# Gated attention and a token/channel mixer on one core: the mixer's work for each batch put into two stretches of fixed contents

## The chip, the cores and the metric

The kernel runs on one core of one Trainium2 chip. A core has five engines with instruction queues of their own: PE (TensorE, matmuls into PSUM), ACT (ScalarE), DVE (VectorE), POOL (GpSimd) and SP (SyncE, which here issues DMAs alone), and 16 DMA engines that all queues share. PSUM is held as bank pairs, of which this kernel uses four in turn. The metric is the time of one execution in microseconds (us) on the device; smaller is better.

## The reference

Eight batches of 3008 rows, 256 wide; z has 64 columns, w_tok1 leads from 3008 rows to 256 tokens and w_tok2 back, w_ch1 leads from 256 to 1536 channels and w_ch2 back.

```python
# for each batch
scores = (1.0 / S) * z @ z.T              # S = 3008
attn   = np.maximum(scores, 0.0) ** 2
x      = u * (attn @ v)
h      = np.maximum(x.T @ w_tok1, 0.0) @ w_tok2
u2     = x + h.T
out    = u2 + np.maximum(u2 @ w_ch1, 0.0) @ w_ch2
```

Each batch's mixer needs the x of the whole batch (x.T @ w_tok1 sums over all rows), so the mixer of a batch can begin only when its attention is finished; the attention of the next batch doesn't wait for it.

## The kernel before

**Tiles and blocks.** The rows of a batch b are cut into six query blocks q of 512 rows (the last has 448), and into six key groups g of four tiles of 128. A block (b, q) needs the squared scores of its six groups. scores are symmetric, so a block that lies above the diagonal is computed once and turned for its mirror: `flips` (L275) says which, `flip` (L515) issues the DMA transpose on SP (L518) from an at tile into an fl tile. From batch 2 on, the diagonal block is scored as a triangle and completed by three small transposes (`flip_tiles`, L508, L511). There are six at buffers and ten fl buffers.

**Attention on PE.** Scores (`score_run`, L424) have 64 rows of contraction, and the product with v (`av_matmul`, L646) is cut into two halves of 64 rows, so both run as two row tiles side by side in the array. ACT applies the relu (`relu`, L450 and L462), DVE squares (`square`, L470; L499 for triangles). At a block's end `finish` copies one half of the sum (ACT, L771), adds the other (DVE, L777), and `gate` (L787) multiplies by u, turned by SP beforehand (L228): that is x, transposed (xT, L798 and L803). `turn_x` (L809, issue at L811) turns it on SP for the mixer.

**The mixer on PE.** Its matmuls use the whole array of 128 rows. For a batch it is cut into pieces (`add_mixer`, L834): six of tok1 (L851, result a_ps, which read x), six of tok2 (L870, h_ps), then 36 of ch1 (L911, hp; four matmuls each, put out to h2pre by ACT at L925 or by DVE at L927) and 23 or 24 of ch2 (L955, op; twelve matmuls each). DVE adds the residual (L971, L989) and SP writes the result out (L976, L992). The residual needs u2 turned by SP (L893). tok1 and tok2 pieces lie in a list `heads`, ch1 and ch2 pieces in a list `tails`; a batch's pieces are added to both lists when its last block ends.

**The order.** It is written out by a planner in the kernel's own Python, before anything runs: a loop (from L1260) keeps an assumed clock for PE and for ACT, DVE and SP, and decides at each step what PE takes next: scores, an attention half, or a mixer piece (L1310 to L1336, else the earliest, L1337 to L1345). What the other engines do is kept in lists (`push`) with an assumed ready time, busy time and latency, and each engine's queue is the order in which the planner takes them. On the chip all queues run in that order and wait for each other by semaphores.

Before the change, a mixer piece is chosen by a budget: time spent on attention earns mixer time (`per_batch`, `flat`, `SLOW`, L1371), pieces spend it, and the run may be overdrawn by `SWING`. A mixer run starts between two blocks, at even q alone, and lasts until the budget is spent or no piece is ready; where none is ready, PE takes scores or an attention half.

**Loads.** POOL issues them. From batch 1 on, u, v and z loads are asked for at fixed steps of the attention (`at_group`, L1112; the step is counted in groups) and let out one by one (`ask_some`, L1123), at least `SPACING` = 4.5 us of assumed PE time apart. Ahead of each stands a one-element copy (`after`, L120) from a recent result, which holds POOL's queue until PE's work has come as far as that. z loads of the next batch are asked for at steps 14 to 19 of 36, v loads from step 28 on. When the third and the sixth z load is out, the turning of z on SP (L137, L141) is put into a list `later`, which u's turns share and which is worked off from its head.

Of the kernel before, what the change touches and what calls it, by code (L numbers as in the profile page):

```python
# [44 lines left out]
class Piece:  # L45


    def __init__(self, cost, needs, fn, opens=False, closes=False, room=None,
                 urgent=False):
        self.cost, self.needs, self.fn = cost, needs, fn  # L50
        self.opens, self.closes, self.room = opens, closes, room
        self.urgent = urgent


@with_exitstack
def kernel(
# [12 lines left out]
    B, S, D = u.shape  # L69
# [398 lines left out]
    def square(unit, view, t):  # L468
        (b, q, g), pr = unit
        nc.vector.tensor_mul(view, view, view)  # L470
        if (b, q, g) in early:
            for e in early[b, q, g][2 * pr:2 * pr + 2]:
                e.t = t
            if pr == 0:
                blocks[b, q, g] = (
                    Done(t), ats[b, q, g].rearrange("p (i w) -> p i w", w=QW), "at", [1])
            else:
                ats.pop((b, q, g))
            return
# [12 lines left out]
        recent[0] = at[:, :1]  # L492
# [212 lines left out]
    def do_half(start, g):  # L705
# [81 lines left out]
    def gate(blk, dh, acc, t):  # L787
# [46 lines left out]
    def add_mixer(b):  # L834
# [164 lines left out]
        for q in range(NQ):  # L999
            heads.append(Piece(0.874, [x_done[b, NQ - 1]], lambda end, q=q: tok1(q, end),  # L1000
                               opens=q < NQ - 1, closes=q > 0))
        for q in range(NQ):
            heads.append(Piece(4 * column_time(widths[q]), [a_done, tok2_done[q]],
                               lambda end, q=q: tok2(q, end)))
        def add_ch1(q, c2):
            h2_done[q, c2] = Done()
            tails.append(Piece(4 * column_time(widths[q]), [u_done[q]] + w_done[:2],
                               lambda end: ch1(q, c2, end),
                               room=("h2", "us") if c2 == 0 else ("h2",)))

# [12 lines left out]
        def add_ch2(q, half, i):  # L1023
            two = not alone(q, half)
            needs = [Sooner(h2_done[q, c2], 0.218 * c2) for c2 in range(CHT // 2)]
            tails.append(Piece(1.312, needs + w_done[2:],
                               lambda end: ch2(q, half, i, end), opens=two and i == 0,
                               closes=two and i == 1))


        early = ROOM["h2"] - CHT // 2
        for q in range(NQ):
            for c2 in range(early if q else 0, CHT // 2):
                add_ch1(q, c2)
            if q + 1 < NQ:
                for c2 in range(early):
                    add_ch1(q + 1, c2)
            for half in halves(q):
                for i in range(pieces_of(q, half)):
                    add_ch2(q, half, i)  # L1040

    def next_piece(t):
# [71 lines left out]

    asks, later = [], []
    last_ask = [0.0]
# [22 lines left out]
    def z_then_turn(b, j):  # L1139
        load_z(b, j)  # L1140
        if j % 3 == 2:
            later.append((pe[0] + 11.0, lambda: True, lambda: turn_next_z(b - 1, j // 3)))

    for b in range(B):
        base = b * NQ * NG
# [8 lines left out]
        if b + 1 < B:  # L1154
            at_group(base + NG, lambda b=b: new_zT(b + 1))
            for j, c in enumerate(vorder):
# [72 lines left out]

    per_batch = 0.87 * NQ * (2 + CHT // 2) + 1.35 * 4 * NQ  # L1230
    flat = NQ * NG * 1.73 + NQ * (NQ + 1) / 2 * 0.44
    fill(7, bank_pair(0, "wp")[:, 0, :])
# [15 lines left out]
    first_u(18.5)  # L1248

    done_units = 2  # L1250
    budget = 8.0
    NOW = 0.05
    STARVED = 0.7
    BACKLOG = 0.9
    GRAIN = 2
    SWING = 2.0
    SPACING = 4.5
    SLOW = 0.84
    LONG = 12.0
    while cur[0] is not None or heads or tails:  # L1260
        run_engines(pe[0])
        ask_some()
        t = pe[0]
        ta, g = next_half(t)
        tm, pieces = next_piece(t)
        blk = cur[0]

# [34 lines left out]

        between = blk is None or blk.acc[0] is None
        mixer_now = tm <= t + NOW and (budget > -SWING or blk is None)
        pick = None
# [31 lines left out]
        if pick is None:  # L1337
            options = [(ta, "av"), (tm, "mixer")]
            if n_now and (whole or low if runs else spare):
                options.append((ts, "scores"))  # L1340
# [26 lines left out]
        else:  # L1367
            if not pieces[0].urgent:
                budget -= pieces[0].cost
            do_piece(tm, pieces)  # L1370
        if pick != "mixer" and blk is not None and blk.b >= 1:  # L1371
            budget += per_batch * (pe[0] - t) / flat * (SLOW if blk.b == 1 else 1.0)
    run_engines(FAR)
# [30 lines left out]
```

## Time and profile before

| what | us |
|---|---|
| median of 3 runs | 1148.66 |
| lowest and highest of them | 1147.0, 1149.11 |
| the profiled execution's own time | 1146.15 |
| its span, first to last instruction | 1144.4 |
| PE busy | 1134.3 |
| DVE busy | 638.4 |
| ACT busy | 548.9 |
| POOL busy | 153.6 |

The page and the views of the trace describe one execution. A row of a group has the line, the engine, the operation, its tiles and shape and its count, then busy time and the mean of one in ns, then the idle time of the engine ahead of it. PE's matmuls overlap and their ends are modelled, so the mean of one (374 ns for 512 columns) is a latency and not a price; starts tell the price. A few matmul records are missing from the trace (for instance 1106 of 1152 at L911), while all weight loads are there.

From the groups, in ns: a relu of a score unit at L462 takes 1028 (a triangle's, in smaller pieces, 441 at L450), a square 687, ch1's evacuation 999 on ACT and 1211 on DVE, the copy at a block's end 579, the add 676, the gate 665, the residual 692.

PE alternates between attention stretches of two blocks and mixer stretches: for batch 4, for instance, an attention stretch runs from 602.4 to 624.05, a mixer stretch to 646.6, an attention stretch to 670.6, a mixer stretch to 696.2. The program ends with one mixer stretch of about 100 us, from 1039.1 on, which holds the rest of batch 6 and all of batch 7.

### The profile page before, as it was taken

Reading aid. Unit: us, or ns where it says so; the run is one execution under the profiler, and the core shown is the slowest. Engines: PE = TensorE matmul, PEld = TensorE weight load, DVE = VectorE, ACT = ScalarE, POOL = GpSimd, SP = SyncE. Lnnn points to the kernel's source line nnn. Section 1 sums busy time; section 2 is a strip of 40 time slices with the busy share of each in tenths; the row PEclk is TensorE's granted clock in tenths of the full one; section 3 lists DMA queues with packets and bytes.
Section 4 is the critical chain, followed back from the end, with each engine's and each line's share of the span. In section 5 each row is a group of like instructions: output and inputs, shape, how many; then the busy total and the mean of one; then the engine's idle time right before and its main releaser. Section 6 shows DMA issues by size and latency. Waiting matters only on the chain.

```text
span 1144.4 us, 22411 instructions
## 1 busy us (share of the span) xinstructions
PE 1134.3 (99%) x9160; PEld 673.0 (59%) x9219; DVE 638.4 (56%) x947; ACT 548.9 (48%) x699; POOL 153.6 (13%) x387
## 2 busy tenths in 40 slices
PE   9999999999999999999999999999999999999998
PEld 3455465645557566565565655665566556566666
DVE  6888454465553755537546375554644656434544
ACT  7998534374352752526525354344543554412331
POOL 4500110210111001111011100111002110000000
PEclk9999999999999999999999999999999999999999
DMA  9999964975879858799688996899867997742122
GB/s 159 191 171 230 164 120 97 203 138 118 170 120 197 164 114 157 132 198 161 122 150 141 186 176 111 152 140 189 164 126 140 151 183 149 121 103 56 51 84 65
DMA packets 468199, 164.85 MB, mean 144 GB/s; under 512 B 431936, under 2 KB 445824, under 8 KB 468096
## 3 DMA queue, kind: packets, MB, share of 16 engines
q1 hardware_dynamic: 440240, 130.72, 57.9%
q0 software_dynamic: 27344, 32.32, 20.9%
q8 instruction: 72, 1.18, 0.4%
q10 hardware_dynamic: 512, 0.38, 0.1%
q14 instruction: 31, 0.25, 0.1%
HBM read 65.40 MB, written 24.64 MB: 79 GB/s over the span
## 4 chain that ended last, share of the span: by engine, by line
PE 97%; DMA 2%; issue 0%; DVE 0%; POOL 0%; SPq 0%; DVEq 0%
PE acc L646 41%; PE op L955 21%; PE hp L911 21%; PE sc L424 6%; PE a_ps L851 4%; PE h_ps L870 4%; DMA v_sb<-in_v_dram 1%; DMA zf<-in_z_dram 1%; DVE h2pre L927 0%; POOL v_sb L206 0%; PE first_acc L563 0%; SPq L159 0%; POOL mark L120 0%; DVE res L989 0%; DVEq L927 0%
## 5 line engine op out<-in xcount | busy, mean ns | idle before, releaser
L646 PEld LDWEIGHTS <-v_sb 64*128 64x128 bf16 x4418 | 238.7, 94 | 223.0 <-issue 4.6
L646 PE MATMUL acc<-at,v_sb 64*128 64x512 bf16 (+1 forms) x2738 | 341.6, 374 | 0.0
L925 ACT ACTIVATE h2pre<-hp 128x1024 bf16<-128x1024 f32 (+1 forms) x161 | 160.7, 999 | 315.2 <-PE hp L911 314.9
L462 ACT ACTIVATE at<-sc 128x1024 bf16<-128x1024 f32 (+1 forms) x294 | 287.8, 1028 | 30.6 <-PE sc L424 25.9
L911 PE MATMUL hp<-xT,w_ch_sb 128*128 128x512 bf16 (+1 forms) x1106 | 254.9, 374 | 2.4
L470 DVE TENSOR_TENSOR at<-at 128x1024 bf16<-128x1024 bf16 (+1 forms) x294 | 200.7, 687 | 99.5 <-ACT at L462 96.0
L955 PE MATMUL op<-w_ch_sb,h2pre 128*128 128x256 bf16 x2208 | 251.4, 273 | 0.3 <-DVE h2pre L927 0.2
L955 PEld LDWEIGHTS <-h2pre 128*128 128x128 bf16 x2208 | 215.4, 98 | 38.0 <-issue 2.2
L927 DVE TENSOR_SCALAR h2pre<-hp 128x1024 bf16<-128x1024 f32 (+1 forms) x127 | 153.8, 1211 | 91.5 <-PE hp L911 91.5
L646 PE MATMUL acc<-fl,v_sb 64*128 64x512 bf16 (+1 forms) x1680 | 195.0, 367 | 0.0
L911 PEld LDWEIGHTS <-w_ch_sb 128*128 128x128 bf16 x1152 | 111.8, 98 | 125.7 <-issue 4.4
L971 DVE TENSOR_TENSOR res<-op,u_sb 128x512 f32<-128x512 f32 x87 | 60.2, 692 | 153.4 <-PE op L955 153.2
L424 PE MATMUL sc<-zT 64*128 64x512 bf16 (+1 forms) x732 | 132.6, 361 | 0.1
L777 DVE TENSOR_TENSOR cp<-acc,cp 128x512 f32<-128x512 f32 (+1 forms) x94 | 63.5, 676 | 101.4 <-ACT cp L771 100.4
L771 ACT COPY cp<-acc 128x512 f32<-128x512 f32 (+1 forms) x89 | 51.5, 579 | 131.3 <-PE acc L646 116.4
L450 ACT ACTIVATE at<-sc 128x512 bf16<-128x512 f32 (+3 forms) x144 | 52.1, 441 | 54.4 <-PE sc L424 43.5
L424 PEld LDWEIGHTS <-zT 64*128 64x128 bf16 x732 | 40.4, 94 | 42.1 <-issue 6.9
L798 DVE TENSOR_TENSOR xT<-cp,uT 128x512 bf16<-128x512 f32 (+1 forms) x94 | 62.5, 665 | 3.1 <-PE hp L911 1.4
L879 DVE TENSOR_TENSOR xT<-xT,h_ps 128x1024 bf16<-128x1024 bf16 (+1 forms) x48 | 55.8, 1174 | 9.4 <-PE h_ps L870 9.3
L120 POOL CAST mark<-at 128x1 f32<-128x1 bf16 x49 | 13.1, 268 | 340.4 <-DVE at L470 340.4
L499 DVE TENSOR_TENSOR at<-at 128x512 bf16<-128x512 bf16 (+3 forms) x144 | 38.1, 321 | 30.1 <-ACT at L450 24.1
L932 POOL COPY hs<-h2pre 128x128 bf16<-128x128 bf16 x48 | 15.6, 325 | 252.6 <-ACT h2pre L925 233.0
(56 smaller groups left out, 342.2 us busy)
## 6 DMA issues: line engine op xcount, KB each, us to landing
out_dram<-res SPq DMA_DIRECT2D x87, 256.0 KB, 2.3
v_sb<-in_v_dram POOLq DMA_DIRECT2D x40, 256.0 KB, 5.9
ur<-in_u_dram POOLq DMA_DIRECT2D x40, 256.0 KB, 5.5
w_tok_sb<-in_moe_w_tok_dram POOLq DMA_DIRECT2D x10, 256.0 KB, 9.4
zs<-in_z_dram POOLq DMA_DIRECT2D x35, 64.0 KB, 3.2
at<-at SPq DMA_TRANSPOSE x108, 2.5
fl<-at SPq DMA_TRANSPOSE x105, 5.5
v_sb<-in_v_dram POOLq DMA_DIRECT2D x8, 192.0 KB, 4.6
```

What stands on the lines that cost most here:

```text
L424: nc.tensor.matmul(sc[:, r, c0:c1], zT[h, k:k + P], zT[h, m + c0:m + c1], start=True, stop=True)
L462: nc.scalar.activation(view, sv, ACT.Relu, scale=inv_S)
L470: nc.vector.tensor_mul(view, view, view)
L646: nc.tensor.matmul(o, vs[blk.b, g][rows, i, dh * P:(dh + 1) * P], rhs, start=(dh, h) not in blk.begun, stop=stop, skip_group_check=True)
L777: nc.vector.tensor_add(cp[:, :W], acc[:, 0, :W], cp[:, :W])
L798: nc.vector.tensor_mul(xT[:, dh, :full * P].rearrange("p (t s) -> p t s", s=P), acc[:, :full * P].rearrange("p (t s) -> p t s", s=P), uT[: ...
L879: nc.vector.tensor_add(to, to, h[:, :, :n * P].rearrange("p h (s t) -> p h t s", t=n))
L911: nc.tensor.matmul(hp[:, r, :W], w_ch1_sb[:, dc, cc * P:(cc + 1) * P], xT[:, dc, :W], start=(dc == 0), stop=(dc == DT - 1))
L925: nc.scalar.activation(h2[:, :, :W], hp[:, :, :W], ACT.Relu)
L927: nc.vector.tensor_single_scalar(h2[:, :, :W], hp[:, :, :W], 0.0, AX.max)
L955: nc.tensor.matmul(op[:, i, :], h2, w_ch2_sb[:, cc, :], start=(cc == 0 and (i == 0 or apart)), stop=(cc == CHT - 1), skip_group_check=True)
L971: nc.vector.tensor_add(res.rearrange("p i (h d) -> p i h d", d=P), op.rearrange("p i (h d) -> p i h d", d=P), us[:, :, half * 2:half * 2 + ...
```

## The change

Each mixer piece gets a key: (its batch, 0) for tok1, (b, 1) for tok2, (b, 2 + q) for the ch1 and ch2 pieces of block q, where ch1 pieces that are made early carry the key of the block in which they are made. A variable `goal` holds the highest key that may run now. It is raised between two blocks alone: ahead of block 0 of batch b (from 2 on) to (b-1, 1), which lets out the rest of batch b-2 and tok1 and tok2 of b-1; ahead of block 3 to (b-1, 4), which lets out the channel pieces of blocks 0 to 2; in batch 1 ahead of block 2 to tok1 and ahead of block 3 to (0, 4); and without limit when no block is left. As long as a piece at or below the goal is left, PE takes the mixer or waits for it; afterwards it takes none. The budget and its constants are gone.

Besides this:
- A mirror's transpose of a block 0 or 3 (batch 2 and later) is not taken by the planner before the x of the block ahead has been.
- The assumed latency of the turning of x is 12.0 us for a batch's last block, 7.5 as before for the others.
- All six z loads are asked for at step 16, all six v loads at step 33; the turns of z have a list of their own, `later_z`.
- A matmul group that belongs to both halves of the columns no longer counts as the final one.

```diff
-                        room=("fl",))
+                        room=lambda: has_room(("fl",)) and (
+                            b < 2 or q % (NQ // 2) or
+                            x_done[divmod(b * NQ + q - 1, NQ)].t is not None))
...
-        final = blk.slot == NG and not any(
+        final = dh is not None and blk.slot == NG and not any(
...
-            push("sp", t, 1.25, 7.5, lambda t: turn_x(b, q, t), first=1)
+            push("sp", t, 1.25, 7.5 if q < NQ - 1 else 12.0, lambda t: turn_x(b, q, t), first=1)
...
+            if not p.urgent and p.key > goal[0]:
+                continue
...
-        while later and later[0][1]() and pe[0] >= later[0][0]:
-            later.pop(0)[2]()
+        for turns in (later, later_z):
+            while turns and turns[0][1]() and pe[0] >= turns[0][0]:
+                turns.pop(0)[2]()
...
-            later.append((pe[0] + 11.0, lambda: True, lambda: turn_next_z(b - 1, j // 3)))
+            later_z.append((pe[0] + 11.0, lambda: True, lambda: turn_next_z(b - 1, j // 3)))
+
+    ZG = 3 * NG - 2
...
-                    at_group(base + 2 * NG + 2 + j,
+                    at_group(base + ZG,
                              lambda b=b, j=j: ask(lambda: z_then_turn(b + 1, j)))
-                    at_group(base + (NQ - 1) * NG - 2 + (j if j > 1 else 0),
+                    at_group(base + (NQ - 1) * NG + 3,
...
+    FIRST, EARLY, LATE = 4, 1, 4
+    goals = {(1, 2): (0, 0), (1, 3): (0, FIRST)}
+    for b in range(2, B):
+        goals[b, 0] = (b - 1, EARLY)
+        goals[b, NQ // 2] = (b - 1, LATE)
...
+        blk = cur[0]
+        if blk is None:
+            goal[0] = (B, 0)
+        elif blk.acc[0] is None:
+            goal[0] = max(goal[0], goals.get((blk.b, blk.q), (-1, 0)))
         tm, pieces = next_piece(t)
-        blk = cur[0]
+        mixing = any(l and l[0].key <= goal[0] for l in (heads, tails))
...
-            if mode[0] == "full" and mixer_now:
-                pick = "mixer"
-            elif mode[0] == "half" and between and mixer_now and (
-                    blk is None or blk.b > 0 and blk.q % 2 == 0):
-                pick = "mixer"
+            if mixing:
+                pick = "mixer" if tm <= t + NOW else None
...
-            elif mixer_now:
-                pick = "mixer"
...
-            options = [(ta, "av"), (tm, "mixer")]
-            if n_now and (whole or low if runs else spare):
+            options = [(tm, "mixer")] if mixing and not runs else [(ta, "av"), (tm, "mixer")]
+            if not mixing and n_now and (whole or low if runs else spare):
                 options.append((ts, "scores"))
```

More of the change, by code (lines that the diff above doesn't have):

```diff
@@ L48, in __init__ @@
     def __init__(self, cost, needs, fn, opens=False, closes=False, room=None,
-                 urgent=False):
+                 urgent=False, key=(0, 0)):
         self.cost, self.needs, self.fn = cost, needs, fn
         self.opens, self.closes, self.room = opens, closes, room
-        self.urgent = urgent
+        self.urgent, self.key = urgent, key
 @with_exitstack
@@ L1000, in add_mixer, with add_ch1 @@
             heads.append(Piece(0.874, [x_done[b, NQ - 1]], lambda end, q=q: tok1(q, end),
-                               opens=q < NQ - 1, closes=q > 0))
+                               opens=q < NQ - 1, closes=q > 0, key=(b, 0)))
         for q in range(NQ):
             heads.append(Piece(4 * column_time(widths[q]), [a_done, tok2_done[q]],
-                               lambda end, q=q: tok2(q, end)))
-        def add_ch1(q, c2):
+                               lambda end, q=q: tok2(q, end), key=(b, 1)))
+        def add_ch1(q, c2, by):
             h2_done[q, c2] = Done()
@@ L1008, in add_ch1 @@
                                lambda end: ch1(q, c2, end),
-                               room=("h2", "us") if c2 == 0 else ("h2",)))
+                               room=("h2", "us") if c2 == 0 else ("h2",),
+                               key=(b, 2 + by)))
         def halves(q):
@@ L1027, in add_ch2 @@
                                lambda end: ch2(q, half, i, end), opens=two and i == 0,
-                               closes=two and i == 1))
+                               closes=two and i == 1, key=(b, 2 + q)))
         early = ROOM["h2"] - CHT // 2
@@ L1033, in add_mixer @@
             for c2 in range(early if q else 0, CHT // 2):
-                add_ch1(q, c2)
+                add_ch1(q, c2, q)
             if q + 1 < NQ:
                 for c2 in range(early):
-                    add_ch1(q + 1, c2)
+                    add_ch1(q + 1, c2, q)
             for half in halves(q):
@@ L1040, in add_mixer @@
                     add_ch2(q, half, i)
+    goal = [(-1, 0)]
     def next_piece(t):
@@ L1113, in at_group @@
         fetch.setdefault(n, []).append(f)
-    asks, later = [], []
+    asks, later, later_z = [], [], []
     last_ask = [0.0]
@@ L1228 @@
         at_group(NG + 1 + k * (NQ * NG - 2 * NG + W_LATER) // len(items), item)
-    per_batch = 0.87 * NQ * (2 + CHT // 2) + 1.35 * 4 * NQ
-    flat = NQ * NG * 1.73 + NQ * (NQ + 1) / 2 * 0.44
     fill(7, bank_pair(0, "wp")[:, 0, :])
@@ L1248 @@
     first_u(18.5)
+    FIRST, EARLY, LATE = 4, 1, 4
[3 more added lines that the diff above has]
+        goals[b, NQ // 2] = (b - 1, LATE)
     done_units = 2
-    budget = 8.0
     NOW = 0.05
@@ L1255 @@
     GRAIN = 2
-    SWING = 2.0
     SPACING = 4.5
-    SLOW = 0.84
-    LONG = 12.0
     while cur[0] is not None or heads or tails:
@@ L1301 @@
         spare = need > t + 1.7 or len(by_then) > 1
-        between = blk is None or blk.acc[0] is None
-        mixer_now = tm <= t + NOW and (budget > -SWING or blk is None)
         pick = None
@@ L1367 @@
         else:
-            if not pieces[0].urgent:
-                budget -= pieces[0].cost
             do_piece(tm, pieces)
-        if pick != "mixer" and blk is not None and blk.b >= 1:
-            budget += per_batch * (pe[0] - t) / flat * (SLOW if blk.b == 1 else 1.0)
     run_engines(FAR)
```

## The prediction, made before the changed kernel was run

> **What bounds the kernel now.** I read the page's first part first, then the chain of work that ended last. TensorE is busy for 99% of the span and makes 97% of the chain, the granted clock is 0.999, and the idle time before every PE group on the page is a few us at most. No wait of another engine can therefore be won back in tens of us: the time is the sum of the matmuls and of what stands between them.
>
> ```profile
> PE 1134.3 (99%) x9160; PEld 673.0 (59%) x9219; DVE 638.4 (56%) x947; ACT 548.9 (48%) x699; POOL 153.6 (13%) x387
> ...
> PE 97%; DMA 2%; issue 0%; DVE 0%; POOL 0%; SPq 0%; DVEq 0%
> ```
>
> So I next read PE's timeline where its work changes kind: attention matmuls and scores run as two 64-row tiles (64*128), the mixer's as the whole array (128*128). I call the two kinds of run an attention stretch and a mixer stretch. The columns are start, length, engine, line. A row's length holds the modelled end of its last matmul, so I use differences of starts.
>
> ```profile
> 620.70 0.94 PE L646 MATMUL acc<-fl,v_sb 64*128 64x448 bf16 x8
> 621.46 0.39 PE L424 MATMUL sc<-zT 64*128 64x512 bf16 x2
> 621.67 2.45 PE L646 MATMUL acc<-fl,v_sb 64*128 64x448 bf16 x24
> 624.05 1.90 PE L911 MATMUL hp<-xT,w_ch_sb 128*128 128x512 bf16 x7
> ```
>
> Eight attention matmuls (four pairs) take 621.46-620.70 = 0.76 us, so a pair takes 0.19. The 24 ahead of the change take 2.38 us for 12 pairs, where 2.28 is due: attention to mixer costs 0.10 us, read to the table's rounding, 0.09 to 0.12.
>
> ```profile
> 638.62 5.40 PE L851 MATMUL a_ps<-x_sb,w_tok_sb 128*128 128x256 bf16 x48
> 643.86 2.78 PE L955 MATMUL op<-w_ch_sb,h2pre 128*128 128x256 bf16 x24
> 646.57 3.63 PE L646 MATMUL acc<-at,v_sb 64*128 64x512 bf16 x32
> ```
>
> Here 48 matmuls of 256 columns take 5.24 us, 0.109 each. The next 24 take 2.71 where 2.62 is due: mixer to attention costs 0.09 us, again 0.08 to 0.11.
>
> **What the Trainium skill says.** "TensorEngine Tiling (Array Packing)", section Key Properties, states that changing the tiling mode drains the TensorE. It gives no price; the trace agrees and gives about 0.1 us each way. "TensorE: Matmul & The Clock Gate", section Back-to-back issue gap, gives N/2.4 + 2.5 ns between warm matmuls: 109 ns for 256 columns, which is what the trace shows, so nothing is left to win inside a stretch. "PSUM — Partial Sum Buffer", section Engine vs sequencer instructions, calls the ScalarE and VectorE queues strict FIFO; this trace does not test it, but it is why I ask below what stands ahead of an evacuation. "DMA: Bandwidth & Descriptors", section Issuing engines are not separate DMA queues, says that transfers from all issuers share the same 16 engines; the stretch with a DMA share of 1.19 below, where some of SP's issues take 4 us instead of 1.3, agrees.
>
> **The change part by part.**
>
> *Fixed contents, two stretches for each batch.* In the order of the matmuls as built, the count of every kind is the same in both programs (4418 attention, 732 scores, 1152 hp, 2256 op, 384 a_ps, 192 h_ps). Only the grouping differs: 60 changes of kind before, 46 after. The first 18 changes, up to 112 us, are the same. Seven round trips go: 7 x (0.10 + 0.09) = 1.3 us, with bounds 7 x 0.17 = 1.2 and 7 x 0.23 = 1.6. I take 1.4. All of it is on PE, so on the path.
>
> *A wait in the last stretch.* One visible wait stands in the long mixer run that ends the program, where an op group follows its hp group at once:
>
> ```profile
> 1073.11 1.25 PE L955 MATMUL op<-w_ch_sb,h2pre 128*128 128x256 bf16 x10
> 1074.53 3.01 PE L955 MATMUL op<-w_ch_sb,h2pre 128*128 128x256 bf16 x26 [0.17 <-DVE h2pre L927]
> ```
>
> Ten matmuls are due 1.09 us and take 1.42: 0.33 lost. After the change an h_ps group stands between this hp and this op, about 0.87 us of cover. What is late next there may take a part; I count 0.2 us won (0 to 0.33).
>
> *Mixer strict while its goal is open.* This adds the possibility that PE waits: before, a late piece let a score or an attention half go first; now neither may. The dangerous places are the starts of stretches. Rows of the attention stretch of batch 4, of the mixer stretch that ends at it and of the one after it (columns: PE, PEld, DVE, ACT, POOL busy, clock, DMA share, GB/s):
>
> ```profile
> 624.05:646.57 22.52, 22.41 (x176) 17.14 (x177) 8.80 (x13) 5.12 (x6) 3.40 (x10) 1.00 1.19 199
> 646.57:670.59 24.02, 24.02 (x225) 11.59 (x225) 14.88 (x28) 18.22 (x25) 1.75 (x4) 1.00 0.92 165
> 670.59:696.18 25.59, 25.48 (x168) 16.34 (x169) 16.70 (x20) 8.35 (x9) 1.54 (x4) 1.00 0.68 137
> ```
>
> ACT is busy 76% and DVE 62% in the attention stretch and PE does not wait. The new attention stretch with 54 scores in three blocks holds 27 score units. From the group rows: ACT 21 x 1.03 + 12 x 0.44 + 6 copies x 0.58 = 30.4 us; PE 282 x 0.108 + 27 x 0.21 = 36.1 us, so 84%. Denser, not full; six at tiles stand ready ahead. I count nothing, up to 0.3 a stretch.
>
> From batch 2 on (six times) the stretch in the middle of a batch opens with eight hp pieces (32 matmuls) directly behind scores; until now a start had at most six. PE gives a piece each 4 x 0.216 = 0.87 us. At its start there are left, by the group rows: ACT the end of a relu and a copy, 1.4 us; DVE two squares, an add and two gates, about 3.0 us. Eight evacuations, four at 1.00 (ACT) and four at 1.21 (DVE), make 8.8. Together 13.2 us on two engines, 6.6 each, while the eighth piece needs the fourth one's bank pair at 7 x 0.87 = 6.1 us. Four evacuations and the backlog are done by about 4.7, so about 1.4 us of slack. Value taken 0; bound above 0.9 us a stretch if two evacuations land on the busier engine.
>
> *x ahead of the mirrors, and 12.0 for its latency.* DVE writes the last of a batch's x here, and SP's timeline follows (the word SPq marks issues):
>
> ```profile
> 625.95 0.22 DVE L803 TENSOR_TENSOR xT<-cp,uT 128x64 bf16<-128x64 f32 x1
> ```
>
>
> ```profile
> 626.23 1.30 SPq L893 DMA_TRANSPOSE u_sb<-xT  x1
> 627.63 4.77 SPq L518 DMA_TRANSPOSE fl<-at  x1
> 632.50 0.53 SPq L976 DMA_DIRECT2D out_dram<-res  x1
> 633.12 1.32 SPq L811 DMA_TRANSPOSE x_sb<-xT  x1
> 634.54 3.87 SPq L518 DMA_TRANSPOSE fl<-at  x1
> ```
>
> x is written at 626.17 and issued 7 us later, behind a mirror transpose (fl) and an output. It takes 5.6 us to land, at 638.7, while a_ps begins at 638.62; only the last eight a_ps matmuls read it, 4.4 us later. So today's slack is 4 us and the reordering wins nothing by itself. After the change x stands ahead of all five mirrors: issued about 3 us into the stretch, landed at 9, while a_ps begins behind hp24, op48 and hp20, 44 x 0.216 + 48 x 0.109 = 14.7 us in. On SP the mirrors, the u turns and outputs queue behind it: the five mirrors at 4 to 5 us each end about 30 us into a stretch of 64 x 0.216 + 180 x 0.109 + 24 x 0.216 = 38.6 us, and their first reader is the second block after it. Cost 0. Without that cover a_ps would wait by the lateness, up to 5 us in each of seven stretches.
>
> *v and z in mixer stretches; z's turns with a list of their own.* The instruction counts on POOL and SP do not change (387 and 502). The sixth v load follows the third output group, about 24 us into the stretch; with 5.9 us to land that is 30 of 38.6. z is turned about half a batch ahead of its first score. POOL's queue behind a load's mark holds hs copies and an xT memset, which in the built order stand after marks that are met earlier. Cost 0 while these leads hold; the gain of emptier attention stretches is also 0, since no DMA ends a PE wait there now. The one-line condition on a matmul group's end (final) changes no count.
>
> **The sum.** The profiled execution took 1146.15 us: span 1144.4 and 1.75 around it. Less 1.4 and 0.2 gives 1144.5. The median of the runs shown, 1148.66, lies 2.5 above that execution; the same step from it gives 1147.0.
>
> **Rivals.**
> 1. *Nothing changes.* Fewer, longer stretches win 1.4 us, and waits of 0.1 us at each of the fourteen stretch starts, where bank pairs change hands, give it back: 1148.5. For it: waits of 0.1 exist in attention stretches. Against it: they are not at starts.
> 2. *Slower.* One mechanism: the eight hp pieces behind scores run out of bank pairs in the six mid-batch stretches that open so, and the strict rule offers no other work. At 0.9 us each 5.4 - 1.6 = 3.8 us more: 1152.5. It decides from 0.65 us a stretch, where the sum reaches +2.3. Against it: 1.4 us of slack by the rows.
> 3. *More than forecast.* The small waits of the old attention stretches (about 0.1 us in every second one) vanish as well and a change costs its upper bound: 1.6 + 0.3 + 0.9 = 2.8, so 1145.9.
>
> **How the numbers follow.** A measurement of this kernel can tell about 0.2%, 2.3 us, from no change, so the bounds are 1146.4 and 1151.0. Forecast 0.60 (of which 0.12 falls below 1146.4, as its spread with the runs' own 1 us is large against the 0.6 us between), no change 0.14, slower 0.14, more 0.12. Faster 0.12 + 0.12 = 0.24; same 0.48 + 0.14 = 0.62; slower 0.14. The range from 1145.2 to 1151.0 leaves out most of the slower case and the lower third of the third rival, 0.16 in all. The forecast's own range is 1146.0 to 1148.2.
>
> **What would show it.** PE busy stays near 1134 and the span falls with the number of changes of kind, each still about 0.1 us. Right on x: its transpose issues within 4 us of the block's end and lands before a_ps. Wrong if PE shows idle time before L911 at a mid-batch start released by h2pre at L925 or L927 (rival 2), before L851 released by x, or before L646 released by v_sb; more than 0.5 us in each stretch overturns the sign.

## The result, and the profile after

| | median us | lowest to highest | runs |
|---|---|---|---|
| before, beside it | 1147.83 | 1146.47 to 1149.11 | 4 |
| after | 1179.77 | 1174.68 to 1190.72 | 4 |

The ratio is 1.0291, with a 95% interval from 1.0217 to 1.0365: the changed kernel is slower, by about 32 us. The forecast said 1.6 us faster. The profiled execution of after took 1178.88 us, of which 1177.1 are its span; before's span was 1144.4, so 32.7 us are to be found.

The page of after; its last line is a group row (busy time, mean of one in ns, then the engine's idle time ahead of it and what ended most of it), and the view below it is the same row before:

```profile
PE 1143.3 (97%) x9162; PEld 666.3 (57%) x9219; DVE 646.0 (55%) x949; ACT 550.9 (47%) x697; POOL 149.1 (13%) x387
...
PE 92%; DMA 5%; ACT 1%; issue 1%; DVE 0%; SPq 0%; ACTq 0%; POOL 0%
...
L424 PE MATMUL sc<-zT 64*128 64x512 bf16 (+1 forms) x732 | 133.7, 365 | 22.5 <-ACT at L462 11.3
```

```profile
L424 PE MATMUL sc<-zT 64*128 64x512 bf16 (+1 forms) x732 | 132.6, 361 | 0.1
```

Two readings account for the loss. PE stands idle for 22.5 us ahead of the scores (L424), where before's row had 0.1. And PE is *busy* 9.0 us longer (1143.3 against 1134.3) with the same matmuls, so some of them ran more slowly. Together 31.4 of 32.7. In the chain the DMA's share rises from 2% to 5%, and 4% of it are mirrors (fl<-at), which before's chain did not hold.

**Where.** By differences of starts, all of it lies in six places: the attention stretches with 54 scores, one in each of batches 2 to 7. They last 40.99, 41.38, 42.00, 39.36, 42.35 and 40.29 us, 246.4 together, where about 35.8 each is due (35.61 was measured later with 52 scores; the two more are 0.2). That is 31.5 over; the mixer stretches behind them last 2.6 longer together. Less about 1.4 for the fourteen changes of kind that are gone and 0.3 in the last stretch (below), this makes 32.4. In no other stretch does PE wait, but for the start of the program, where it waits for v 0.9 us longer than before.

**One of the six**, batch 4's (530.12 to 572.12). PE's timeline near its end:

```profile
563.77 0.27 PE L424 MATMUL sc<-zT 64*128 64x256 bf16 x2
563.86 1.04 PE L648 MATMUL acc<-fl,v_sb 64*128 64x512 bf16 x8
569.87 0.61 PE L424 MATMUL sc<-zT 64*128 64x512 bf16 x2 [4.96 <-ACT at L450]
570.25 1.94 PE L648 MATMUL acc<-at,v_sb 64*128 64x512 bf16 x8
```

PE stops for 4.96 us ahead of the last score unit. The releaser is ACT's relu (L450), which empties the score's bank. But the relu was itself waiting, for a DMA, as ACT's timeline shows; the view below it is the chain, followed back from there (start, length, what):

```profile
568.84 0.98 ACT L450 ACTIVATE at<-sc 128x512 bf16<-128x512 f32 x2 [5.25 <-DMA fl<-at]
```

```profile
557.50 1.92 PE acc L648 x18
559.42 9.31 DMA fl<-at
...
568.84 0.16 ACT at L450
...
569.87 0.61 PE sc L424 x2
```

The relu needs an at buffer to write into, and the one that it waits for is still being *read* by a mirror's transpose (fl<-at) that takes 9.31 us from issue to landing. Its issue is in SP's timeline; the second view cuts out the first of the two mirrors:

```profile
545.20 1.32 SPq L228 DMA_TRANSPOSE uT<-ur  x1
546.61 3.54 SPq L813 DMA_TRANSPOSE x_sb<-xT  x1
550.24 2.51 SPq L520 DMA_TRANSPOSE fl<-at  x1
552.85 4.71 SPq L513 DMA_TRANSPOSE at<-at  x3
557.66 8.01 SPq L520 DMA_TRANSPOSE fl<-at  x2
565.76 1.26 SPq L228 DMA_TRANSPOSE uT<-ur  x1
```

```profile
557.66 1.66 SPq L520 DMA_TRANSPOSE fl<-at  x1
```

The first mirror takes 1.66 us to issue, the second, from 559.42 on, 6.25. Between the two POOL does this:

```profile
558.50 0.18 POOL L120 CAST mark<-at 128x1 f32<-128x1 bf16 x1 [12.80 <-DVE at L470]
558.99 0.53 POOL L218 DMA_DIRECT2D ur<-in_u_dram  x1 [0.30 <-issue]
```

The u load of the third block (256 KB) is let out at 558.99. The x transpose at 546.61 that took 3.54 to issue also stands behind a u load, the second block's, at 545.17. The Trainium skill, "DMA: Bandwidth & Descriptors", section Issuing engines are not separate DMA queues, says that transfers of all issuers interleave on the same 16 engines. The order of these events fits that; the experiments test it.

**Why PE is also slower.** Windows of the same stretch (PE, PEld, DVE, ACT, POOL busy, clock, DMA share, GB/s): up to the wait, the wait, what follows it, and the rest:

```profile
560.00:564.80 4.80, 4.80 (x48) 2.57 (x45) 1.38 (x2) 1.94 (x2) 0.71 (x2) 1.00 0.83 109
564.80:569.87 5.07, 0.10 (x3) 0.00 (x1) 0.40 (x2) 1.03 (x3) 0.00 (x0) 0.97 1.25 217
569.87:572.95 3.08, 2.86 (x12) 0.94 (x13) 2.68 (x8) 2.38 (x5) 0.00 (x0) 0.50 0.88 197
572.95:580.00 7.05, 7.05 (x36) 3.46 (x36) 5.32 (x6) 4.10 (x4) 0.71 (x2) 1.00 0.72 140
```

Behind the wait the granted clock is 0.50. Such a spell of half clock goes with each of the six waits (3.36, 3.73, 4.96, 2.86, 3.93 and 3.29 us). It lasts 3.41 us in five of them and 6.83 in batch 6; PE is busy for 21.1 us of these spells and loses half of that, 10.5 us. This is the longer busy time: 1143.3 is 10.9 above that of experiment 4 (1132.4, below), which has the two stretches and no such spell, and 9.0 above that of before, whose order is busy 1.9 longer. With the half clock a wait costs about one and a half times its length (34.1 us over in these stretches and those behind them, for 22.4 of waits).

**What had covered this before.** The kernel before makes the same kind of dense stretch, but of two blocks, and behind it:

```profile
507.06:531.08 24.02, 24.02 (x226) 11.59 (x225) 14.88 (x28) 18.21 (x25) 1.75 (x4) 1.00 0.89 160
531.08:556.22 25.14, 24.98 (x159) 15.56 (x161) 16.63 (x19) 8.35 (x9) 2.17 (x6) 1.00 0.66 136
```

The second row is a mixer stretch, 25 us in which no score asks for an at buffer and SP catches up. The delay itself was there too. In before, x's transpose takes 4.17 us to issue behind another u load (issued at 522.16), and nobody on PE was waiting:

```profile
523.49 4.17 SPq L811 DMA_TRANSPOSE x_sb<-xT  x1
```

### The profile page after: what moved, and what is told of

It reads as the page before. It is cut to its first block, busy times and chain, and to the rows that moved or that the text cites. A ratio compares the mean times of both kernels' runs of the same rounds, so it can differ in the third digit from the quotient of the medians.

```text
span 1177.1 us, 22437 instructions
## 1 busy us (share of the span) xinstructions
PE 1143.3 (97%) x9162; PEld 666.3 (57%) x9219; DVE 646.0 (55%) x949; ACT 550.9 (47%) x697; POOL 149.1 (13%) x387
## 4 chain that ended last, share of the span: by engine, by line
PE 92%; DMA 5%; ACT 1%; issue 1%; DVE 0%; SPq 0%; ACTq 0%; POOL 0%
PE acc L648 37%; PE op L957 21%; PE hp L913 21%; PE sc L424 6%; DMA fl<-at 4%; PE a_ps L853 4%; PE h_ps L872 3%; ACT at L462 1%; PE first_acc L565 1%; DMA zf<-in_z_dram 1%; DMA v_sb<-in_v_dram 0%; ACT at L450 0%; DVE xT L881 0%; DVE xT L800 0%; DVE h2pre L929 0%
## 5 line engine op out<-in xcount | busy, mean ns | idle before, releaser
L648 PEld LDWEIGHTS <-v_sb 64*128 64x128 bf16 x4418 | 230.6, 95 | 232.8 <-issue 8.3
L648 PE MATMUL acc<-at,v_sb 64*128 64x512 bf16 (+1 forms) x2738 | 345.5, 378 | 0.0
L929 DVE TENSOR_SCALAR h2pre<-hp 128x1024 bf16<-128x1024 f32 (+1 forms) x129 | 156.6, 1214 | 108.1 <-PE hp L913 108.1
L424 PE MATMUL sc<-zT 64*128 64x512 bf16 (+1 forms) x732 | 133.7, 365 | 22.5 <-ACT at L462 11.3
L450 ACT ACTIVATE at<-sc 128x512 bf16<-128x512 f32 (+3 forms) x144 | 53.1, 441 | 75.1 <-PE sc L424 61.3
L424 PEld LDWEIGHTS <-zT 64*128 64x128 bf16 x732 | 41.8, 95 | 68.6 <-issue 31.1
L872 PE MATMUL h_ps<-w_tok_sb,a_sb 128*128 128x512 bf16 (+1 forms) x177 | 47.1, 374 | 0.9
```

Of the source, the lines that this page charges most:

```text
L424: nc.tensor.matmul(sc[:, r, c0:c1], zT[h, k:k + P], zT[h, m + c0:m + c1], start=True, stop=True)
L648: nc.tensor.matmul(o, vs[blk.b, g][rows, i, dh * P:(dh + 1) * P], rhs, start=(dh, h) not in blk.begun, stop=stop, skip_group_check=True)
L872: nc.tensor.matmul(h[:, dh, :W], st["a"][:, th, dh * P:(dh + 1) * P], w_tok2_sb[:, th, q * QW:q * QW + W], start=(th == 0), stop=(th == 1))
L929: nc.vector.tensor_single_scalar(h2[:, :, :W], hp[:, :, :W], 0.0, AX.max)
```

## The experiments

The theory: the u load of the third block meets the last mirrors' transposes on the DMA engines, these end late, and the scores of the third block need the at buffers that they read at once, since no mixer stretch lies between any more. Rivals: the hold that puts x ahead of the mirrors; the moved v and z loads; too few at buffers. All ratios are against the kernel before, run on the same chip, with 95% intervals. Unless said otherwise the edit is to the changed kernel.

**1. The u load of the third block out of the way**, asked for in the mixer stretch behind z's first load; in batch 7, where no z load exists, it stays.

```diff
-                else:
+                elif q != 2 or b + 1 == B:
                     at_group(base + q * NG + 2, lambda m=m: ask(lambda: u_then_turn(m)))
...
+                    if j == 0:
+                        at_group(base + ZG, lambda m=b * NQ + 4: ask(lambda: u_then_turn(m)))
```

> The u load that the changed kernel issues in the third block of the 54-score attention stretch is asked for behind the first z load instead, so in the mixer stretch; the matmuls of that stretch keep their order. Theory A (the mirrors' transposes get slow because this load shares the DMA engines with them, and so hold the at tiles that the next scores need): the waits of 3 to 5 us before scores fall to under 1 us in each of the six stretches, the time falls from about 1179 to 1150-1158. Theory B (three blocks without a mixer stretch ask more of SP's transposes than it can issue, with or without the load): under a third is won back, 1170-1179.

Measured 1155.87 us, ratio 1.0079 [1.0064, 1.0094]: 24 of the 32 us are gone. The order of PE's work in these stretches is unchanged. The waits fall to between 1.0 and 1.8 us in batches 2 to 6, not below 1 us as theory A expected, while batch 7, whose load was left, keeps its own. Batch 4's, then batch 7's:

```profile
556.08 0.37 PE L424 MATMUL sc<-zT 64*128 64x512 bf16 x2 [1.53 <-ACT at L462]
```

```profile
985.66 0.39 PE L424 MATMUL sc<-zT 64*128 64x512 bf16 x2 [3.95 <-ACT at L450]
```

One kernel thus holds the case and its control. What is left may have its own load: the first z load, 64 KB, now goes out 28.9 to 29.3 us into the stretch, where the u load stood, and the mirror beside it takes 2.4 to 3.4 us to issue.

**2. Three short stretches for each batch**, so that mixer work comes after every second block, and the hold is on the mirrors of blocks 0, 2 and 4.

```diff
-                            b < 2 or q % (NQ // 2) or
+                            b < 2 or q % 2 or
...
-    goals = {(1, 2): (0, 0), (1, 3): (0, FIRST)}
+    goals = {(1, 2): (0, 3), (1, 4): (0, 5)}
...
-        goals[b, NQ // 2] = (b - 1, LATE)
+        goals[b, 2] = (b - 1, 3)
+        goals[b, 4] = (b - 1, 5)
```

> Fixed contents, but three mixer stretches for each batch (ahead of blocks 0, 2 and 4), the hold on mirrors at those blocks; loads as in the changed kernel. Theories A and B: with two blocks in a row SP catches up in every mixer stretch, no wait over 0.5 us before scores, time within 3 us of the kernel before, 1146-1151. Theory C (the fixed contents, the strict rule or the moved loads cost the time, not the number of blocks in a row): 1165 or more.

Measured 1156.25 us, 1.0079 [1.0064, 1.0094]. The time missed the expectation, but the wait on at buffers did vanish: none is left ahead of scores. Other waits came, because this cut puts tok2 directly behind tok1:

```profile
661.41 2.76 PE L872 MATMUL h_ps<-w_tok_sb,a_sb 128*128 128x512 bf16 x11 [0.69 <-ACT a_sb L860]
```

With shorter ones ahead of op (up to 0.5) and in the attention (0.2), the trace has 7.2 us of such waits, of the 9 us by which this run is slower than before. So the run supports the lost cover and says nothing on what a good cut in three would take.

**3. Without the hold.**

```diff
-                        room=lambda: has_room(("fl",)) and (
-                            b < 2 or q % (NQ // 2) or
-                            x_done[divmod(b * NQ + q - 1, NQ)].t is not None))
+                        room=("fl",))
```

> The hold on the mirrors of blocks 0 and 3 is undone alone; the matmul order of the 54-score stretch stays the same. Theories A and B: the waits stay, 1172-1185, since the late mirrors are those of blocks 1 and 2, which no hold touches. Theory C (the hold moves mirrors into the attention stretch): 1150-1160.

Measured 1180.24 us, 1.0293 [1.0255, 1.033], and the waits stay at 3.8 to 4.5 us. The hold isn't the cause.

**4. The planner told that a mirror takes longer.** It assumed 6.5 us from a mirror's taking to its landing; in batch 3 the decisive mirror landed 37 us into the stretch in the trace, some 7 us behind the plan.

```diff
-            done = push("sp", t, 1.8, 6.5, lambda t: flip(b, q, g, at, uses, done),
+            done = push("sp", t, 1.8, 10.0, lambda t: flip(b, q, g, at, uses, done),
```

> The planner assumes 10.0 us instead of 6.5 from a mirror transpose's issue to its landing, so it counts an at tile as free later and puts scores behind attention matmuls. Theories A and B: the last scores of the stretch move behind about two groups of attention matmuls, the waits shrink by about that, 2 us in each of six stretches with the slow clock after them, 1155-1168. If the at tiles are not what the scores wait for, nothing changes: 1175-1183.

Measured 1144.2 us, 0.9975 [0.9961, 0.9989]: below the kernel before, and below both expectations, since the waits went altogether. The page of this run:

```profile
PE 1132.4 (99%) x9162; PEld 665.6 (58%) x9219; DVE 642.7 (56%) x949; ACT 549.3 (48%) x697; POOL 153.1 (13%) x387
...
PE 98%; DVE 1%; issue 0%; ACT 0%
...
L424 PE MATMUL sc<-zT 64*128 64x512 bf16 (+1 forms) x732 | 132.3, 361 | 0.1
```

The idle time ahead of scores is back at 0.1. In batch 4's stretch, now 35.61 us and without a gap, two things differ. It holds 52 scores instead of 54, in another order; and the mark that lets the third block's u load out comes earlier in POOL's queue:

```profile
518.04:553.65 35.61, 35.61 (x335) 18.46 (x335) 21.38 (x41) 25.33 (x37) 2.99 (x7) 1.00 0.93 161
```

```profile
543.23 0.53 POOL L218 DMA_DIRECT2D ur<-in_u_dram  x1 [0.29 <-issue]
```

```profile
545.77 3.89 SPq L520 DMA_TRANSPOSE fl<-at  x2
```

The load is let out 25.2 us into the stretch (28.9 in after), and both last mirrors are issued behind it, 1.9 us each, landing 4.2 and 4.7 us later. The last lands at +34.4, not +38.6. Right beside the load stand two of the small at<-at now: they take 1.2 us to issue, as they do without a load, and land after 4.5 and 3.5, and PE waits for neither. Which of the two differences counts is asked in 13 and 14.

**5. The u loads of the second and third block out of the way** (as in 1, for both).

```diff
-                else:
+                elif q not in (1, 2) or b + 1 == B:
...
+                    if j < 2:
+                        at_group(base + ZG, lambda m=b * NQ + 3 + j: ask(lambda: u_then_turn(m)))
```

> As the run with one u load moved, but the u loads of the second and third block both leave the 54-score stretch for the mixer stretch (not in the last batch, whose loads stay). Theory A (SP falls behind the plan because a transpose beside a u load takes 4 to 5 us to issue; each of the two loads adds to the lag): the 1.4 to 1.9 us that were left before the last scores fall below 0.5 us in batches 2 to 6, and 4 us stay in batch 7; time 1146-1151. Theory B (the number of transposes alone): they stay at 1.4 to 1.9 us, time 1154-1158.

Measured 1150.43 us, 1.0031 [1.0019, 1.0042]. In batches 2 to 6 PE no longer waits for scores at all, as theory A expected. But these stretches now hold 56 scores in another order, and the first z load comes 32.4 us into them, behind the last mirrors. So it is not shown that what experiment 1 had left over was the lag from the second block's load. Batch 7, in the order of the changed kernel, again keeps its wait:

```profile
978.78 0.39 PE L424 MATMUL sc<-zT 64*128 64x512 bf16 x2 [3.79 <-ACT at L450]
```

**6. Seven at buffers, nine fl.**

```diff
-    ROOM = {"at": 6, "fl": 10, "xT": 9, "x": 7, "h2": 8, "us": 2}
+    ROOM = {"at": 7, "fl": 9, "xT": 9, "x": 7, "h2": 8, "us": 2}
```

> Seven at tiles instead of six, nine fl tiles instead of ten (there is no room for both); u loads as in the changed kernel. Theories A and B, in which the scores wait for an at tile that a late mirror still reads: with a tile more PE has about one group of four score tiles, 2 us, more of lead, but the planner spends the tile on earlier scores; the waits fall by 0 to 3 us each, time 1155-1180. If at tiles don't matter: the same as the changed kernel, 1175-1183.

Measured 1175.06 us, with single runs from 1166.8 to 1197.5, 1.0221 [1.0169, 1.0273]: waits of 1.2 to 3.3 us remain, and the last mirrors still take 5.0 to 6.3 us to issue beside the third block's load. Both expectations hold this time. The stretches have 56 scores here and one mirror buffer fewer, so the run doesn't isolate the count. It shows only that this trade doesn't cure it.

**7. v and z loads where they were before.**

```diff
-                    at_group(base + ZG,
+                    at_group(base + 2 * NG + 2 + j,
...
-                    at_group(base + (NQ - 1) * NG + 3,
+                    at_group(base + (NQ - 1) * NG - 2 + (j if j > 1 else 0),
```

> The z and v loads are asked for at the old steps (14 to 19, and from 28 on), all else as changed. Theory A: z loads of 64 KB then come beside the transposes of the 54-score stretch as well and the u loads come later, so the waits stay or shift, 1160-1190. Theory C (the moved loads are what costs the time): back to 1146-1152.

Measured 1185.91 us, 1.034 [1.0321, 1.0358]: not better, rather worse. The order of whole stretches changes with it and the waits spread. Taking back the move of the loads does not take back the loss.

**8. The kernel before with 10.0** (the edit of 4, in the kernel before).

> The kernel before with the planner's 10.0 us for a mirror's landing alone. If the gain of the changed kernel with 10.0 us comes from fewer changes of kind, this stays within 0.3% of the kernel before, 1145-1151. If 10.0 us is by itself a better plan, it gains as much: 1143-1145.

Measured 1149.57 us, 1.0027 [1.001, 1.0043]. The constant gains nothing by itself in the old order. Set against this run, that of 4 gains 5 to 6 us, more than the 1.6 that the forecast had for fewer changes of kind; but with 10.0 the old order has six changes more than before, so the two are not quite alike.

**9. 8.0 in place of 10.0.**

```diff
-            done = push("sp", t, 1.8, 6.5, lambda t: flip(b, q, g, at, uses, done),
+            done = push("sp", t, 1.8, 8.0, lambda t: flip(b, q, g, at, uses, done),
```

> 8.0 us for a mirror's landing in the plan, between the changed kernel's 6.5 and the 10.0 that won. In the changed kernel the mirror that the last scores wait for lands about 7 us later than the plan has it. Theory A: at 8.0 the plan is still some 5 us short at that place, part of the scores move, waits of 1 to 3 us stay in the six stretches, 1150-1168. If any shift of the scores would do: 1143-1146.

Measured 1146.26 us, 0.9983 [0.997, 0.9997]. Theory A was wrong here: the last four score units stand where the changed kernel has them (one unit has left the stretch, and some in its middle stand up to a group elsewhere), and yet three of the six stretches are only 0.3 to 0.5 us over and the others not at all. What did move was the mark of the u load, 40 matmuls earlier. That turned the question from the order of the scores to the place of the load.

**10. 10.0 without the hold** (the edits of 3 and 4 together).

> The winning version without the hold on mirrors, to see what the hold is worth. a_ps begins 14 us into its stretch and x landed 5 to 10 us later without the hold, still ahead of a_ps: no difference above 0.2%, 1142-1147. If the hold carries the gain: 1150 or more.

Measured 1144.55 us, 0.9977 [0.9964, 0.999]; no difference from 4 that can be measured.

**11. 10.0 with the old places of the loads** (the edits of 4 and 7 together).

> The winning version with the z and v loads at the old steps, to see what moving them is worth once at tiles are planned late enough. Theory A: more loads stand beside the transposes in attention stretches and SP falls further behind, waits come back in part, 1148-1175. If the moved loads are worth nothing: 1142-1147.

Measured 1190.13 us, 1.0368 [1.0334, 1.0402], slower than either expectation. PE's waits in it (who waits for whom, us in total, times, longest):

```profile
PE sc L424 <- ACT at L462: 22.2, 18, 3.6
PE acc L648 <- DMA at<-at: 3.8, 4, 1.6
```

With two stretches, the old places of the v and z loads cost some 45 us against experiment 4; that part of the change is needed by the other. By which transfer each of these waits arises, and those of experiment 7, was not followed further.

**12. The kernel of 4 once more.**

> The winning version once more, beside the two others on the same chip: 46 changes of kind instead of 60 and no wait in their place, 1143-1146, 0.1% to 0.4% below the kernel before.

Measured 1145.24 us, 0.9981 [0.9969, 0.9994].

**13 and 14. The place of the load alone.** In 13 the changed kernel asks for the third block's u load one step earlier, and the order of PE's work in the 54-score stretch is identical to it (the mark stands at matmul 206 of the stretch, not 254). In 14 the kernel of 4 asks for it two steps later (276, not 214), with its order of PE's work. The edit shown is that of 13; 14 has a 4 in place of the 1, besides the 10.0.

```diff
-                    at_group(base + q * NG + 2, lambda m=m: ask(lambda: u_then_turn(m)))
+                    at_group(base + q * NG + (1 if q == 2 else 2), lambda m=m: ask(lambda: u_then_turn(m)))
```

> Only the u load of the third block is asked for one group earlier, whose mark then is the at tile of the 207th instead of the 255th matmul of the 54-score stretch; the matmuls of that stretch stand exactly as in the changed kernel. Theory A (the meeting of this load and the last mirrors costs the time): waits before the last scores fall from 3-5 us to at most 2 us, time 1144-1158. Theory D (the order of the last scores costs it, and 10.0 us won because it moved them): no gain, 1172-1185.

> The version with 10.0 us, where the same load's mark moves from the 215th to the 277th matmul of the stretch, all matmuls of that stretch in the order that won. Theory A: the load meets the last mirrors again, waits of 2 us and more come back, 1155-1180. Theory D: it stays at 1143-1147.

| | load at its own place | load moved |
|---|---|---|
| order of the changed kernel | 1179.8 | 1150.1, ratio 1.0024 [1.0013, 1.0036] (earlier) |
| order with 10.0 | 1144.2, 1145.2 | 1151.6, ratio 1.0038 [1.0014, 1.0063] (later) |

In 13 the waits shrink to 0.5 to 1.6 us a stretch, in batch 7 to nothing, and the clock isn't lowered after them. Batch 4 has the most, in two waits:

```profile
554.77 0.37 PE L424 MATMUL sc<-zT 64*128 64x512 bf16 x2 [0.64 <-ACT at L462]
...
557.86 0.39 PE L424 MATMUL sc<-zT 64*128 64x512 bf16 x2 [0.92 <-ACT at L450]
```

So with not one matmul of these stretches moved, the place of one load is worth 30 us. The first z load, next in POOL's queue, goes out 4 to 9 us earlier with it, but batch 7, which has no z load, loses its wait as well.

The some 5 us between 13 and 4 come with the other order of the scores, and were not taken apart. 14 took a time between its two expectations and doesn't settle that order's part: in its trace the load goes out 31.1 us into the stretch, 0.7 to 1.9 us after the issue of the last mirror has begun, so the meeting of the changed kernel, a load just ahead of the last mirror, is not made again. It shows that a load moved that late costs this order about 7 us. (The profiled execution of 14 took 1169 us, far above its median, so nothing is read from its waits.)

## Why the prediction was wrong, point by point

**The step that failed** is the one headed "Mixer strict while its goal is open": of the new stretch with 54 scores it says "Denser, not full; six at tiles stand ready ahead. I count nothing, up to 0.3 a stretch". The runs showed 2.9 to 5.0 us of wait and 1.4 to 2.5 us lost to half clock in each of the six. The sum there (ACT 84% of PE's time) was a sum of busy times, and ACT's load was not what failed: in experiment 4 the stretch runs with ACT at 25.33 of 35.61 us, 71%, and no gap. What the step left out is who holds the at buffers. A buffer is free not when its scores are squared but when SP's mirror has read it. In batch 4 that was 38.6 us into the stretch, and the relu of the last scores asks at 33.5 (568.84 less the 5.25 us that ACT waited).

**A question asked of the wrong tile.** On the mirrors queued behind x the prediction priced a delay by "their first reader is the second block after it. Cost 0". For those mirrors the 0 came true: experiments 3 and 10 take the hold away, and nothing changes. But it asked who reads the mirror (fl), not who waits for the buffer that the mirror reads (at), and so it didn't see the mirrors of the blocks inside the stretch. It took 4 to 5 us of SP for each; the decisive one held SP for 6.25 and landed after 9.31. It had the sign before it: the 4.77 and 3.87 us to issue that it set against the 1.3 of an x turn are mirrors, which take about 1.6 with no load beside them.

**A cover that was not named.** "No DMA ends a PE wait there now" was true of before, and gave the emptier attention stretches a worth of 0. With two stretches and 10.0 they are worth some 45 us (experiment 11 against 4). In before a mixer stretch followed the second block; the change takes just this away, and the prediction never asked what it had covered. Experiment 2, which puts it back, has no wait ahead of scores.

**The rivals.** None was the one that came, and no sign of being wrong named scores (L424). The slower one (bank pairs at the mid-batch start) did not occur. In experiment 4, where no wait comes before it, the start looks like this:

```profile
552.66 1.06 PE L648 MATMUL acc<-at,v_sb 64*128 64x512 bf16 x8
553.65 7.08 PE L913 MATMUL hp<-xT,w_ch_sb 128*128 128x512 bf16 x31
560.57 2.67 PE L957 MATMUL op<-w_ch_sb,h2pre 128*128 128x256 bf16 x23
```

Thirty-two hp matmuls (one record is missing) take 560.57 - 553.65 = 6.92 us, 0.216 each: no piece waited for a bank pair, and the forecast's 0 was right. Its slack of 1.4 us does not follow from its terms, though: two squares, an add and two gates make 3.4 us by the rows, not 3.0, so DVE's second evacuation ends at 5.8, 0.3 ahead of the 6.1. Where this start did wait, up to 3.2 us in experiment 6 and 0.4 in 9, it waited for the relu of the last scores (L450) and not for h2pre.

**What was right.** *Changes of kind*: in the lines above four pairs of 0.216 and a change take 0.99, so the change costs 0.13; over the stretches of after that had no wait it is 0.12 to 0.13, near the 0.1 used. *The last stretch*: with the same matmuls it lasts 100.22 us instead of 100.56; 0.2 was forecast, 0.34 came. *x*: it was to be issued about 3 us into the stretch and landed at 9, with a_ps at 14.7. In batch 5, whose mixer stretch starts at 637.81, x was issued 2.1 us into it, landed at 4.8, and a_ps began at 14.6:

```profile
639.90 1.23 SPq L813 DMA_TRANSPOSE x_sb<-xT  x1
```

```profile
652.45 2.78 PE L853 MATMUL a_ps<-x_sb,w_tok_sb 128*128 128x256 bf16 x24
```

*v and z*: behind the start of the program no PE wait of after ends with a v or z load. *The sum itself*: experiments 4 and 12 have the two stretches without the wait, and both intervals, [0.9961, 0.9989] and [0.9969, 0.9994], hold the forecast's 1147.0 / 1148.66 = 0.9986. They have another order of scores too, and experiment 8 puts the gain at the same constant at 5 to 6 us, so the agreement may in part be luck.

**What stays open.** The share of the half clock in the loss is read from the trace alone; it was not tried apart from the wait. Nor was the number of at buffers by itself, what is left in experiment 1, how a load holds up the transposes beside it, the better order of scores apart from the load's place, or the cause of each wait in 7 and 11.

The best version is that of 4: the change with 10.0 us as the assumed latency of a mirror, faster than both kernels.

## What to carry to other kernels

Before a stretch of covering work is taken away, list every buffer that a slow reader holds (here a DMA that reads at) and ask when it comes free at the latest and who wants it next: busy shares don't show it, and "nobody waits for it now" only holds with the cover in place. An order that is planned ahead is as good as its assumed latencies at the crowded moments: here one mirror in each of six stretches took 7.1 to 9.3 us where 6.5 was assumed, and the kernel lost 2.9%. When the time moves after such a change, look at where one load stands against the transposes beside it before rearranging the matmuls.

## What the runs showed of the hardware

A load from DRAM often holds up a DMA transpose between SBUF buffers that is issued beside it. In the trace of after, from 200 us on, 21 mirrors had no load beside them: their issue held SP for 1.3 to 3.2 us (median 1.6), and they landed after 3.6 to 5.3 (median 3.7). Twelve were issued while a u load of 256 KB was under way: 1.7 to 6.3 us (median 3.2), landing after 5.1 to 9.3 (median 6.4). For the 39 with a v or z load alone beside them the medians are 2.2 and 6.8. It is not so each time: in experiment 4, 2.5 us behind the load, two mirrors took 1.9 to issue and landed after 4.2 to 4.7.

PE's clock can fall after a single wait, and where the wait lies counts as well as its length. The Trainium skill, "TensorE: Matmul & The Clock Gate", section "Part 1: The HAM clock gate", gives half the clock after at least one idle window of about 3.4 us; in the trace a partly idle window is enough. The six spells of half clock in after begin at 275.99, 422.76, 569.53, 716.31, 856.25 and 1006.44 us, which are 43, 43, 43, 41 and 44 times 3.413 us apart: the clock is set anew on a fixed grid of 3.41 us. Batch 5's wait of 2.86 us ended at 715.24 and lay with 2.34 us in the window that ends at 716.31, where the clock fell. In experiment 3 the wait of 3.91 us in the same batch lay across two windows, 1.97 and 1.93 us in each, and the clock stayed whole. After's two windows, then experiment 3's three (columns: span, PE busy, clock, DMA share, GB/s):

```profile
712.90:716.31 3.41, 1.07 (x10) 1.00 1.26 254
716.31:719.72 3.41, 3.19 (x9) 0.50 0.67 149
```

```profile
712.79:716.20 3.41, 1.44 (x16) 1.00 1.25 218
716.20:719.62 3.42, 1.48 (x11) 1.00 1.06 235
719.62:723.03 3.41, 3.36 (x17) 1.00 1.09 155
```

Over all kept traces, from 60 us on, the windows at full clock part at about 2 us: the 49 with 1.0 to 1.98 us of idleness were followed by full clock, the 32 with 1.98 to 3.41 us by half clock. Once the clock was down, less kept it there: batch 6's spell is twice as long, and PE was idle for 1.81 us of its first window.
